# Values of six more blocks' late rows in the opening, and first-MLP products of two token groups in the slots that this frees

## The chip, the cores and the metric

The kernel runs on one core of one Trainium2 chip. A core has a matrix engine (PE), a vector engine (DVE), a scalar engine (ACT), a general engine (POOL), a sync engine that issues most transfers (SP), and 16 DMA engines. The metric is the device time of one execution in microseconds (us); three runs of the kernel before gave 797.42, 798.40 and 799.69 us, median 798.4.

## The reference

A recurrent attention layer over segments, then an MLP, on 2048 tokens of width 512 in bf16:

```python
h  = x  + A(_layernorm(x))      # A: 64 segments of 32 tokens, 32 heads of 128, 8 memory tokens
h2 = h  + B(_layernorm(h))      # B: layernorm, w1 (512x1792), gelu, w2 (1792x512)
# A, for segment s:
hcat = concat([mem, xs])        # 8 + 32 rows
q, k, v = hcat@Wq, hcat@Wk, hcat@Wv        # each 512 -> 32*128
p = softmax(mask(q k^T * 128**-0.5))       # memory columns always seen, the rest causal
o = (p v) @ Wo                              # 4096 -> 512
mem = o[:, :8]; out rows = o[:, 8:]
```

Segment s+1 needs `mem` of segment s, so the 64 segments form a chain. What does not depend on `mem` can be computed at any time before its use.

## The kernel before

All work is recorded as operations with estimated durations; a list scheduler in the program then sets the order on each engine, and semaphores follow from it. The order on PE is written by hand: per segment a table `ORDERS` of parts (Q, K, V passes, scores SC, values times weights PV, output projection WO, scores for the token rows SA), with one filler part `F`. `START` is the hand-written order for segment 0, the opening, in which the four weights (4 MB each) arrive from DRAM in the order WV, WK, WQ, WO.

Of each segment's 32 rows the first 24 sit beside the 8 memory rows in the tile `hT`. The last 8 rows ("late rows") of four segments together form a block's 32 late rows; they do not depend on memory. A block is four segments (16 blocks, `bk = s // 4`, `sg = s % 4`). The late rows' keys, queries and values are made by passes of their own: a pass multiplies 32 rows by 2048 weight columns in 16 matmuls, so values of one block are two passes. The opening makes them for blocks 0 and 1. For the later blocks `part_F2`, the filler of each segment, makes those of block `bk + 2`: keys in `sg` 0, queries in 1, values in 2; `sg` 3 holds the output projection of the late rows (`wo_B`). Values leave PSUM to `VSB`, go to the DRAM tensor `v_last` (`v_B_spread`) and return to `VBD` in another layout (`v_B_gather`).

In blocks 14 and 15 no late rows are left, so the six free fillers hold the start of the MLP: `w1_pair(p, banks)` makes two 128-wide column groups (`fc`) of the first MLP product for the first 512 tokens (token group k=0). There are 14 column groups, seven pairs; pairs 0 to 5 are in these slots, pair 6 comes after the last segment. Their w1 columns are loaded early (`w1_early`, by the table `EARLY`), the products stay in SBUF where tiles are free (`gT0_home`), and `gelu` runs on them in place once the last softmax is done.

After the segments the MLP runs over token groups k = 0 to 3 of 512 tokens: `p2_w1` (128-wide column group, four matmuls of 512 columns) with gelu on ACT, and `p2_w2` (four matmuls per column group). The tiles of WK, WQ and WV are then reused for w1, w2, gelu results, layernormed rows. `p2_load` reads the rows h of a group from DRAM, `p2_norm` and `p2_T` normalize and transpose them (DMA transposes), `p2_res` adds the bias on POOL, `nat(bk)` brings a block's attention output into rows. POOL folds the two halves of `wo_B` (`fold`). All these transfers stand in one in-order queue, SP's.

The program also spaces transfers around PE's instruction fetches and pads PE's instruction stream (`windows`, `pads`); both are computed anew for every version.

## Time and profile before

| what | value |
|---|---|
| median of three runs | 798.4 us (797.42 to 799.69) |
| the profiled execution, device time | 797.54 us |
| its span, first to last instruction | 795.8 us |
| mean granted PE clock | 0.993 |
| PE busy | 765.4 us, 96% of the span |
| DVE, ACT, POOL busy | 585.3, 530.0, 308.1 us |
| moved by DMA | 48.02 MB |

The span falls into three stretches: the opening to 51.7 us (weights arrive, segment 0), the segments 1 to 63 to about 696 us, and the MLP. A number after L is a line of the kernel before; `high` and `quad` are the two halves of PSUM. In the rows of PE, `128*32` is the stationary operand and the number behind `x` counts matmuls; four matmuls with 32 stationary columns each run side by side. Idle time of PE is what can be won without taking work away from it; the profile names for each such wait what ended it.

### The profile page before, as it was taken

The numbers are of one execution on the slowest core, as the hardware profiler recorded it, in microseconds if no ns is written. First come the engines' busy times: TensorE is split into PE (matmuls) and PEld (weight loads), VectorE is DVE, ScalarE is ACT, GpSimd is POOL, SyncE is SP. The second block draws the span as 40 slices with busy tenths as digits, with TensorE's granted clock in tenths as the row PEclk, the third lists the DMA queues.
The fourth block names the chain that finished last, engine by engine and source line by source line (L and its number), as shares of the span: only waits on it lengthen the run. The fifth ranks groups of instructions, "written<-read, shape, count | busy, mean of one in ns | idle before, by whom it ended". The sixth has DMA issues, their size and how long they took to land.

```text
span 795.8 us, 45330 instructions
## 1 busy us (share of the span) xinstructions
PE 765.4 (96%) x19686; PEld 424.7 (53%) x20409; DVE 585.3 (74%) x1862; ACT 530.0 (67%) x1380; POOL 308.1 (39%) x831
## 2 busy tenths in 40 slices
PE   3789999999999999999999999999999999989998
PEld 1345555565665555555555555565655566544443
DVE  4258788888888888888888888888888787834111
ACT  2447777777777777677777777777677677743432
POOL 3013223434343444444444444444452434335600
PEclk9989999999999999999999999999999999999999
DMA  9951000010102010201010101010103211274300
GB/s 338 395 182 24 17 14 26 18 44 11 44 10 57 4 47 14 45 17 38 23 38 23 38 25 36 25 38 23 37 21 80 56 31 44 80 211 106 80 26 27
DMA packets 65056, 48.02 MB, mean 60 GB/s; under 512 B 28500, under 2 KB 61276, under 8 KB 64860
## 3 DMA queue, kind: packets, MB, share of 16 engines
q1 hardware_dynamic: 64528, 44.85, 19.6%
q8 instruction: 158, 2.59, 1.4%
q10 hardware_dynamic: 332, 0.27, 0.2%
q14 instruction: 38, 0.31, 0.1%
HBM read 31.08 MB, written 8.13 MB: 49 GB/s over the span
## 4 chain that ended last, share of the span: by engine, by line
PE 90%; SPq 5%; DMA 2%; DVE 1%; issue 1%; ACT 0%; DVEq 0%
PE high L957 33%; PE high L700 17%; PE quad L1287 15%; PE quad L1677 6%; PE high L1670 5%; PE high L1326 3%; SPq L860 2%; SPq L878 2%; PE quad L1140 2%; PE quad L1197 2%; PE quad L1247 2%; PE quad L1171 1%; PE high L1171 1%; PE high L1487 1%; DMA WO<-in_A_Wo_dram 1%; DMA WQ<-h_mid 1%
## 5 line engine op out<-in xcount | busy, mean ns | idle before, releaser
L957 PE MATMUL high<-WQ,hT 128*32 128x512 bf16 x1796 | 157.5, 383 | 1.6 <-DVE hT L1293 1.0
L700 PE MATMUL high<-WK,hT 128*32 128x512 bf16 x1260 | 126.4, 379 | 0.1
L1220 POOL TENSOR_TENSOR PA<-SA,rsa 128x256 bf16<-128x256 f32 x64 | 39.6, 619 | 219.9 <-DVE rsa L1212 152.6
L1287 PE MATMUL quad<-WO,OT 128*32 128x256 bf16 x4032 | 122.1, 273 | 0.0
L957 PE MATMUL high<-WV,hT 128*32 128x512 bf16 x1528 | 115.9, 380 | 0.0
L976 ACT ACTIVATE kq<-high 128x512 bf16<-128x512 f32 x160 | 94.1, 597 | 22.6 <-PE high L957 19.0
L975 ACT CAST kq<-high 128x512 bf16<-128x512 f32 x161 | 93.7, 582 | 21.5 <-PE high L957 19.8
L1287 PEld LDWEIGHTS quad<-WO,OT 128*32 128x32 bf16 x4032 | 102.3, 97 | 5.0 <-issue 0.2
L1228 POOL COPY BD<-PTA 32x128 f32<-32x128 f32 x256 | 78.3, 306 | 16.3 <-DVE PTA L1224 0.6
L957 PEld LDWEIGHTS high<-WQ,hT 128*32 128x32 bf16 x1796 | 52.0, 95 | 54.8 <-issue 22.9
L998 DVE STREAM_TRANSPOSE KALL<-kq 128x256 f32<-128x256 f32 x160 | 69.3, 433 | 9.7 <-ACT kq L975 7.0
L975 ACT CAST VS<-high 128x512 bf16<-128x512 f32 x126 | 73.1, 580 | 0.1
L955 PEld LDWEIGHTS <-hT 128*32 128x32 bf16 x3248 | 53.1, 97 | 35.1 <-DVE hT L1293 7.0
L1673 ACT ACTIVATE WQ<-high,b1t 128x512 bf16<-128x512 f32 x42 | 28.9, 687 | 54.6 <-PE high L1670 54.6
L975 ACT CAST OT<-quad 128x384 bf16<-128x384 f32 (+1 forms) x126 | 47.3, 375 | 26.3 <-PE quad L1175 25.2
L1299 DVE STREAM_TRANSPOSE TT<-quad 128x256 f32<-128x256 f32 x63 | 28.3, 450 | 42.0 <-PE quad L1287 41.5
L1034 ACT COPY KALL<-KALL 128x128 f32<-128x128 f32 x63 | 18.8, 298 | 58.9 <-PE quad L1197 58.7
L1339 POOL TENSOR_TENSOR opT<-TTB,TTS 32x64 bf16<-32x64 f32 x128 | 40.3, 315 | 40.6 <-DVE opT L1293 22.8
L998 DVE STREAM_TRANSPOSE QT<-kq 128x256 f32<-128x256 f32 x128 | 54.5, 426 | 2.0 <-ACT kq L976 1.8
L957 PE MATMUL high<-WK,hT 128*32 128x512 bf16 x788 | 55.1, 379 | 0.0
L1140 PEld LDWEIGHTS quad<-KALL,ZC 128*32 128x32 bf16 x1984 | 31.2, 96 | 41.3 <-POOL BD L1228 17.4
L700 PE MATMUL high<-WV,hT 128*32 128x512 bf16 x520 | 53.1, 379 | 0.0
(188 smaller groups left out, 1612.3 us busy)
## 6 DMA issues: line engine op xcount, KB each, us to landing
WV<-in_A_Wv_dram SPq DMA_DIRECT2D x4, 1024.0 KB, 10.1
WK<-in_A_Wk_dram SPq DMA_DIRECT2D x4, 1024.0 KB, 18.3
WQ<-in_A_Wq_dram SPq DMA_DIRECT2D x4, 1024.0 KB, 17.6
WO<-in_A_Wo_dram SPq DMA_DIRECT2D x16, 256.0 KB, 7.9
v_last<-VSB SPq DMA_DIRECT2D x60, 64.0 KB, 2.3
VBD<-v_last SPq DMA_DIRECT2D x60, 64.0 KB, 2.0
h_mid<-xr SPq DMA_DIRECT2D x16, 128.0 KB, 2.0
WQ<-h_mid SPq DMA_DIRECT2D x4, 512.0 KB, 5.7
```

What stands on the lines that cost most here:

```text
L700: return e.add_instruction(mybir.InstMatmult(name="I-%d" % (4000000 + _kept[0]), engine=mybir.EngineType.PE, start_tensor_calc=start, stop ...
L955: e.ldweights(l, tile_position=(0, 32 * j))
L957: ins = e.matmul(o, l, m, start=(k == 0), stop=(k == DC - 1), tile_position=(0, 32 * j), skip_group_check=True)
L975: return {"act": (lambda e: e.copy(out, src), t_act(n, ps_)), "dve": (lambda e: e.tensor_copy(out, src), 0.155 + 1.0e-3 * n * fast)}
L976: return {"act": (lambda e: e.mul(out, src, scale_), t_act(n, ps_)), "dve": (lambda e: e.tensor_scalar(out, src, scale_, None, ALU.mult), ...
L998: S.op("dve", lambda e: e.transpose(out, src), reads=[("kq", i)], writes=[key], dur=t_dve(256) + 0.02)
L1140: ins = e.matmul(o[32 * j:32 * j + 32, :], zc_window(h), rhs, start=False, stop=(i == 3), tile_position=(0, 32 * j), skip_group_check=True)
L1228: S.narrow(S.op("pool", lambda e, j=j, rows=rows: e.tensor_copy(words(BD[rows, par, :, j, :, :]), words(PTA[rows, 0:4])), reads=["PTA"], w ...
L1287: ins = e.matmul(ps[bank][32 * j:32 * j + 32, 0:256], lhs(slot(h)), wo_cols(h, b), start=(k == 0), stop=(k == 15), tile_position=(0, 32 * ...
L1339: return e.tensor_tensor(o[32 * q:32 * q + 32, c:c + 2], x, y, ALU.add)
L1670: ins = e.matmul(ps[bank][:, 0:SBT], W1[:, cc, fc * P:(fc + 1) * P], hnT_of(k)[:, cc, :], start=(cc == 0), stop=(cc == DC - 1))
L1677: S.op("pe", lambda e: e.matmul(quad[:, t, c0:c0 + w], gT_of(k, fc)[:, t * P:(t + 1) * P], W2[:, fc, c0:c0 + w], start=(fc == (0 if k else ...
```

## The change

The values of blocks 2 to 7 are made in the opening as well (12 more passes, all from WV), and `part_F2` then makes those of block `bk + 8`. The value slots of blocks 8 to 13 become free: with the six of blocks 14 and 15 there are twelve slots. They take all seven pairs of token group 0 and five pairs (10 of 14 column groups) of token group 1. The products no longer stay in SBUF: each pair is copied to `kq[4:6]`, stored to a DRAM tensor `g_pre` (256 KB) and loaded back after the last segment. Before the values of blocks 2 to 6 can go to DRAM they wait in tiles that are free early (`stages`); the transfers follow in segments 2 to 6.

The late rows of four blocks are now loaded together as one tile (`load_xl`, `ln_late`, tiles `hL`), the ring `hT` holds 3 blocks and not 4, `xr` 5 and not 6, `VS` 2 segments and not 3, `BD` and `BDL` one and not two. `ln1` runs two blocks ahead and not three. The normalized rows of group 0 get a tile of their own, `hn0`, filled around segments 24 to 32; those of group 1 are made around segments 53 to 56.

After the segments, group 0 has only its second product, and group 1 four column groups of the first (10 to 13) and its second product; groups 2 and 3 are as before.

```diff
+VL = 8
+SLOTS = tuple(s for s in range(4, 64) if s % 4 < 3 and s // 4 + (VL if s % 4 == 2 else 2) >= 16)
+NP1 = len(SLOTS) - 7
+EARLY = {2: (("vs", 4, 0.1),), 3: (("vs", 2, 0.1),), 4: (("vs", 3, 0.1),), 5: (("vs", 5, 0.1), ("xl", 3, 0.5)), 6: (("vs", 6, 0.1),),
...
-        RBLK = 4
+        RBLK = 3
...
-        XR = 6
+        XR = 5
...
-        VS = sb("VS", [P, 3, 2, 512])
+        VS = sb("VS", [P, 2, 2, 512])
...
-        BD = sb("BD", [P, 2, 4, 4, SEG, 2])
-        BDL = sb("BDL", [P, 2, 2, 8, 8])
+        BD = sb("BD", [P, 4, 4, SEG, 2])
+        BDL = sb("BDL", [P, 2, 8, 8])
...
         load_x(0, first)
+        load_xl(0, first)
...
-        load_x(1, first)
+        load_xl(1, first)
         load_w(WV, wv_d, "WV")
         load_w(WK, wk_d, "WK")
-        load_x(2, load)
         load_w(WQ, wq_d, "WQ")
...
-        load_x(3, load)
...
+        stages = {1: (halves(opT[:].rearrange("p a c t -> p (a c t)")), [("opA", p_, k) for p_ in range(2) for k in range(4)] + [("opB", p_) for p_ in range(2)]),
+                  2: (halves(xr[:, 3:5, :].rearrange("p a d -> p (a d)")), [("xr", 3), ("xr", 4)]),
+                  3: (halves(TTB[:].rearrange("p c q t -> p (c q t)").bitcast(BF16)), ["TTB"]),
+                  4: (halves(OTB[:, 1].rearrange("p h t -> p (h t)")), [("OTB", 1, sg) for sg in range(4)]),
+                  5: (halves(h0[:, 0:1024]), [("hn0", "a")]),
+                  6: (halves(h0[:, 1024:2048]), [("hn0", "b")])}
...
             def part_F2():
                 banks = BANK["F0"], BANK["F1"]
-                to = bk + AHEAD - 1
                 what = (1, 2, 0)[sg - 1] if bk == 0 else sg
+                to = bk + (VL if what == 2 else AHEAD - 1)
...
-                    w1_pair(3 * (to - NTB) + what, banks)
+                    w1_pair(SLOTS.index(s), banks)
...
-            g, gkeys = gT0_home[p]
-            for n in range(2):
-                S.either(copy2(g[:, n, :], ps[banks[n]][:, 0:SBT], SBT), reads=[("ps", banks[n])], writes=[("W1o", n), ("gT0", 2 * p + n)] + gkeys)
+            o = kq[:, 4:6].rearrange("p i a e b -> p i (a e b)")
+            for a in range(2):
+                S.either(copy2(o[:, a, :], ps[banks[a]][:, 0:SBT], SBT), reads=[("ps", banks[a])], writes=[("W1o", a), ("kq", 4 + a)])
+            S.dma(lambda e: e.dma_start(gd[k, p], o.rearrange("p a n -> p (a n)")), 256, reads=[("kq", 4), ("kq", 5)], writes=[("gd", k, p)])
...
+        for p in range(NP):
+            gT_load(0, p)
+            f = slice(2 * p, 2 * p + 2)
+            S.dma(lambda e, f=f: e.dma_start(W2[:, f], w2_d[:, f]), 256, writes=[("W2", p)], after=used["WK"])
+        p2_load(0)
...
+        for p in range(NP1):
+            gT_load(1, p)
+        w1_load(1)
+        p2_load(1)
+        w1_load(0)
...
-        w1_pair(NP - 1, early)
-        for fc in range(FC):
-            gelu(fc)
+        for fc in range(FC):
+            gelu(0, fc)
         wo(NS, later, mem=False)
-        rest = {0: lambda: nat(NTB - 2), 1: lambda: (pv_a(NS - 1), pv_a_ev(NS - 1)), 3: lambda: (wo_B(NTB - 1, later), fold(14)), 5: lambda: (wo(NS + 1, 7, mem=False), nat(NTB - 1))}
+        rest = {0: lambda: nat(NTB - 2), 1: lambda: (pv_a(NS - 1), pv_a_ev(NS - 1)), 4: lambda: (wo_B(NTB - 1, later), fold(14)), 6: lambda: (wo(NS + 1, 7, mem=False), nat(NTB - 1))}
...
+        for fc in range(2 * NP1):
+            gelu(1, fc)
+        p2_norm(2)
+        p2_T(2)
...
+        for fc in range(2 * NP1, FC):
+            p2_w1(1, fc)
+        for fc in range(FC - lag):
+            p2_w2(1, fc)
+        finish(1)
+        for k in (2, 3):
```

The order of instructions at three places, before and after. PE in the opening, before (`XX` holds the late rows; L957 is a pass of 16 matmuls per half, L905 a transpose, L1076 the turn of block 0's values, L1140 scores):

```order
L957 MATMUL high<-WV,XX 32x512 x32
L957 MATMUL high<-WK,XX 32x512 x32
L957 MATMUL high<-WK,hT 32x512 x32
L957 MATMUL high<-WK,XX 32x512 x32
L957 MATMUL high<-WQ,XX 32x512 x16
L905 MATMUL quad<-ident,XX 128x128 x4
L957 MATMUL high<-WQ,hT 32x512 x16
L957 MATMUL high<-WQ,XX 32x512 x16
L957 MATMUL high<-WQ,hT 32x512 x16
L1140 MATMUL high<-KALL,ZC 32x64 x32
```

and after, from the turn of block 0's values on (L979 is the pass, L913 the transpose; `XX` holds the late rows of blocks 0 to 3, `hL` those of blocks 4 to 7):

```order
L1116 MATMUL quad<-VSB,OTB 128x256 x16
L979 MATMUL quad<-WV,XX 32x512 x32
L979 MATMUL high<-WK,XX 32x512 x16
L979 MATMUL high<-WK,hT 32x512 x16
L979 MATMUL high<-WK,XX 32x512 x16
L913 MATMUL quad<-ident,XX 128x128 x4
L979 MATMUL quad<-WV,hL 32x512 x32
L979 MATMUL high<-WK,XX 32x512 x16
L979 MATMUL high<-WK,hT 32x512 x16
L979 MATMUL high<-WK,XX 32x512 x16
L979 MATMUL quad<-WV,hL 32x512 x48
L979 MATMUL high<-WQ,hT 32x512 x16
```

Value passes now stand between the passes that need the weights which arrive later. PE at the end of the segments, before (L1326 is `wo_B`, L1487 `w1_pair`, L1287 WO, L1677 the second MLP product, L1247 and L1253 the last values times weights):

```order
L1287 MATMUL quad<-WO,OT 32x256 x64
L1326 MATMUL high<-WO,OTB 32x512 x16
L1487 MATMUL high<-XX,hT 32x512 x16
L1487 MATMUL high<-XX,xr 32x512 x16
L1287 MATMUL high<-WO,OT 32x256 x64
L1677 MATMUL quad<-WK,xr 128x512 x4
L1247 MATMUL high<-BD,VS 128x2x32 x16
L1253 MATMUL high<-BDL,VBD 128x8x8 x4
L1677 MATMUL quad<-WK,xr 128x512 x4
L1677 MATMUL quad<-WK,VSB 128x512 x4
L1326 MATMUL high<-WO,OTB 32x512 x32
```

and after (L1366 is `wo_B`, L1327 WO, L1735 the second product, L1287 and L1293 the last values times weights, L1728 the first product):

```order
L1327 MATMUL quad<-WO,OT 32x256 x64
L1366 MATMUL high<-WO,OTB 32x512 x16
L1327 MATMUL high<-WO,OT 32x256 x64
L1735 MATMUL quad<-WK,WQ 128x512 x4
L1287 MATMUL high<-BD,VS 128x2x32 x16
L1293 MATMUL high<-BDL,VBD 128x8x8 x4
L1735 MATMUL quad<-WK,WQ 128x512 x12
L1366 MATMUL high<-WO,OTB 32x512 x32
L1735 MATMUL quad<-WK,WQ 128x512 x8
L1327 MATMUL high<-WO,OT 32x256 x64
L1735 MATMUL quad<-WK,WQ 128x512 x32
L1728 MATMUL high<-XX,WK 128x512 x16
```

Pair 6 is gone from between `wo_B` and WO, the next `wo_B` has one column group of the second product more ahead of it, and only 16 matmuls of the first product follow for group 1. SP's queue at the same place, before (L1688 loads w2, L1693 w1, L1421 rows of h, L1438 transposes rows, L1357 is `nat`):

```order
L1695 DMA WQ<-in_B_b_dram 128x512
L1688 DMA WK<-in_B_w_dram 128x2x512 x5
L1421 DMA WQ<-h_mid 128x2048
L1688 DMA WK<-in_B_w_dram 128x2x512 x2
L1693 DMA WK<-in_B_w_dram 128x896
L1438 DMA_TRANSPOSE WQ<-WV 128x4x128 x4
L1693 DMA WK<-in_B_w_dram 128x896 x3
```

and after (L1522 loads the stored products, L1765 w2, L1745 w1, L1458 rows of h, L1397 is `nat`):

```order
L1522 DMA WQ<-g_pre 128x1024 x6
L1765 DMA WK<-in_B_w_dram 128x2x512 x5
L1522 DMA WQ<-g_pre 128x1024
L1765 DMA WK<-in_B_w_dram 128x2x512 x2
L1745 DMA WK<-in_B_w_dram 128x896 x4
L1458 DMA WQ<-h_mid 128x2048
L1767 DMA WQ<-in_B_b_dram 128x512
L1522 DMA KALL<-g_pre 128x1024 x4
L1397 DMA_TRANSPOSE oN<-opT 128x4x128
L1522 DMA KALL<-g_pre 128x1024
L1745 DMA WK<-in_B_w_dram 128x896 x3
L1458 DMA WQ<-h_mid 128x2048
```

Six loads of 256 KB now stand ahead of the first load of w2, and the rest of group 1's products, half of w1 and the rows of groups 1 and 2 stand behind `nat` of block 14.

More of the change, by code (lines that the diff above doesn't have):

```diff
@@ new lines, in build_kernel, with w1_home, w1_early @@
+        homes = [(VSB[:].rearrange("p i r e -> p (i r e)"), [("VSB", 0), ("VSB", 1)]),
+                 (QTB[:, 13 % AHEAD].rearrange("p h t b -> p (h t b)"), [("QTB", 13 % AHEAD, r) for r in range(2)])]
+        def w1_home(n):
+            late = sum(s >= NS - 7 for s in SLOTS[:n + 1])
+            v, keys = homes[late % 2]
+            return v.rearrange("p (c f) -> p c f", c=DC), keys
+        def w1_early(n, after):
+            v, keys = w1_home(n)
+            p = n % NP
+            for c in range(DC):
+                S.dma(lambda e, c=c: e.dma_start(v[:, c, :], w1_d[:, c, 2 * p * P:(2 * p + 2) * P]), 64, writes=[("W1p", n, c)], after=after + S.users(keys))
@@ new lines, in gT_key, with gT_load, gelu @@
+        def gT_key(k, fc):
+            return ("gT1" if k == 1 else "gT", fc)
+        def gT_load(k, p):
+            o = gT[:, 2 * p:2 * p + 2, :] if k == 0 else KG[:, 2 * p:2 * p + 2, :]
+            S.dma(lambda e: e.dma_start(o.rearrange("p a n -> p (a n)"), gd[k, p]), 256, reads=[("gd", k, p)], writes=[gT_key(k, 2 * p + n) for n in range(2)], after=used["KG"] if k else used["WQ"])
+        def gelu(k, fc):
+            g, key = gT_of(k, fc), gT_key(k, fc)
+            start = k == 0 and fc == 0
+            S.op("act", lambda e: e.activation(g, g, ACTF.Gelu_apprx_tanh, bias=b1t[:, fc:fc + 1], scale=1.0), reads=[key, "b1t"], writes=[key],
+                 dur=0.65 + 1.1 * start, after=[S.last_writer["SA"], S.last_writer[("EC", 1)]] + ([] if start else [S.last_writer[("gT", 0)]]))
@@ L1559, in tail @@
                 if folds:
-                    fold(n, behind + [S.last_writer[("BD", s % 2, j)] for j in range(4 * (s == NS - 1))])
-                if turned and s % 4 == 3:
+                    fold(n, behind + [S.last_writer[("BD", j)] for j in range(4 * (s == NS - 1))])
+                if turned and (s % 4 == 3 or s == NS - 10):
                     for f in turned:
@@ L1646, in build_kernel @@
                 tail(0)
-                chain += spread["out", 1] + spread["in", 1]
+                load_xl(2, load)
+                load_x(1, load)
+                chain += spread["out", 1] + spread["in", 1] + spread["out", VL - 1]
                 for a_, b_ in zip(chain, chain[1:]):
@@ L1663, in build_kernel @@
             used[key] += S.users([(key, r, c_) for r in range(2) for c_ in range(DC)])
+        used["KG"] = S.users([("KA", p_, r) for p_ in range(2) for r in range(2)] + [("KB", p_, r) for p_ in range(AHEAD) for r in range(2)] + [("KL", p_) for p_ in range(2)])
+        used["QG"] = S.users([("QTB", p_, r) for p_ in range(AHEAD) for r in range(2)])
         def p2_w1(k, fc):
@@ L1727, in build_kernel @@
                 for c in range(parts):
-                    for fc in (range(FC - lag, FC) if k else ORDER0[FC - lag:]):
+                    for fc in range(FC - lag, FC):
                         p2_w2t(k, fc, t, c * w, w)
                     cols = slice(c * w, c * w + w)
-                    S.op("dve", lambda e, t=t, bf=bf, cols=cols: e.tensor_tensor(ob[:, bf, t, cols], quad[:, t, cols], hb[:, bf, t, cols], ALU.add),
-                         reads=[("ps", t), ("hb", bf, t)], writes=[("ob", bf, t, c)], after=used["WV"], dur=t_dve(w))
@@ new lines, in build_kernel @@
+        wo(NS, later, mem=False)
+        rest = {0: lambda: nat(NTB - 2), 1: lambda: (pv_a(NS - 1), pv_a_ev(NS - 1)), 4: lambda: (wo_B(NTB - 1, later), fold(14)), 6: lambda: (wo(NS + 1, 7, mem=False), nat(NTB - 1))}
+        p2_res(0)
+        p2_load(2)
+        for fc in range(FC - lag):
+            rest.get(fc, lambda: None)()
+            p2_w2(0, fc)
+        finish(0)
+        for fc in range(2 * NP1):
+            gelu(1, fc)
+        p2_norm(2)
+        p2_T(2)
+        p2_res(1)
+        p2_load(3)
@@ L1734, in build_kernel @@
+        for fc in range(2 * NP1, FC):
+            p2_w1(1, fc)
+        for fc in range(FC - lag):
+            p2_w2(1, fc)
+        finish(1)
+        for k in (2, 3):
+            for fc in range(FC):
+                p2_w1(k, fc)
+                if fc >= lag:
+                    p2_w2(k, fc - lag)
+                if fc == 8:
+                    p2_res(k)
+                if fc == 8 and k == 2:
+                    p2_norm(3)
+                    p2_T(3)
+            finish(k)
         S.op("sp", lambda e: e.nop(), reads=[("out", tb, c) for tb in range(NTB) for c in range(1 + (tb == NTB - 1))])
```

272 lines of the change are left out of this document (129 added, 143 removed), and 7 rows, old and new, of tables (EARLY, START).

## The prediction

> **What bounds the kernel now.** I read the page's busy times and slices first, then what PE waited for in each of the three stretches, then the chain of work that ended last in the opening.
>
> ```profile
> span 795.8 us, 45330 instructions
> PE 765.4 (96%) x19686; PEld 424.7 (53%) x20409; DVE 585.3 (74%) x1862; ACT 530.0 (67%) x1380; POOL 308.1 (39%) x831
> PE   3789999999999999999999999999999999989998
> PEclk9989999999999999999999999999999999999999
> GB/s 338 395 182 24 17 14 26 18 44 11 44 10 57 4 47 14 45 17 38 23 38 23 38 25 36 25 38 23 37 21 80 56 31 44 80 211 106 80 26 27
> ```
>
> PE is the bound from the fourth slice on: only the first three slices, in which 338 and 395 GB/s of weights come in, leave it idle, and one near the end. A matmul that leaves the later slices is worth its full time; one put into the first slices may be free. The waits, by stretch (0 to 52, 52 to 690 and 690 to 796 us, in this order):
>
> ```profile
> PE high L957 <- DMA WQ<-in_A_Wq_dram: 3.5, 3, 2.0
> PE high L957 <- DMA WK<-in_A_Wk_dram: 1.5, 1, 1.5
> ...
> PE high L1487 <- DMA VSB<-in_B_w_dram: 1.7, 1, 1.7
> PE quad L1197 <- issue: 1.4, 6, 0.3
> ...
> PE high L1287 <- issue: 0.8, 1, 0.8
> PE high L1326 <- DVE OTB L975: 0.7, 1, 0.7
> ```
>
> In 638 us of segments PE waits a few us, and 1.7 of them once, for the w1 columns of the first pair. In the opening it is the reverse, and there the chain shows what ends it:
>
> ```profile
> 40.20 8.04 DMA WO<-in_A_Wo_dram
> ...
> 50.41 0.36 PE high L1287 x8
> ...
> 51.72 0.39 PE high L957
> ```
>
> Up to 48.2 us the chain is WO arriving; segment 1 begins at 51.72. PE work added before that point moves the end only if PE is then later than WO.
>
> **The change, part by part.** *What leaves the MLP.* PE from the last segment on:
>
> ```profile
> 696.87 1.04 PE L1487 MATMUL high<-XX,hT 128*32 128x512 bf16 x16
> 697.74 1.04 PE L1487 MATMUL high<-XX,xr 128*32 128x512 bf16 x16
> 698.60 0.71 PE L1287 MATMUL high<-WO,OT 128*32 128x256 bf16 x17
> ...
> 709.46 1.93 PE L1287 MATMUL high<-WO,OT 128*32 128x256 bf16 x64
> ...
> 719.11 4.66 PE L1670 MATMUL high<-WQ,WK 128*128 128x512 bf16 x19
> 723.60 1.03 PE L1677 MATMUL quad<-WK,WQ 128*128 128x512 bf16 x4
> ...
> 725.33 1.03 PE L1677 MATMUL quad<-WK,WQ 128*128 128x512 bf16 x4
> ```
>
> From 723.60 to 725.33 PE does one column group of the second product and one of the first, so a group is 0.865 us. Ten groups of token group 1 leave: 8.65 us. Pair 6 leaves the place between 696.87 and 698.60: 1.73 us. Both lie on the path. In the freed slots a pair replaces the two value passes of a block, which take as long:
>
> ```profile
> 21.55 1.91 PE L957 MATMUL high<-WV,XX 128*32 128x512 bf16 x32
> 23.28 1.47 PE L957 MATMUL high<-WK,XX 128*32 128x512 bf16 x24
> ```
>
> 21.55 to 23.28 is 1.73 us for a block's values. So the segments keep their length, and the added work of six blocks is 6 x 1.73 = 10.4 us, all in the opening.
>
> *What the opening has room for.* By stretches (PE busy is the second time, the granted clock the third number from the end):
>
> ```profile
> 17.00:27.00 10.00, 7.58 (x120) 3.77 (x104) 2.23 (x4) 3.98 (x9) 0.00 (x0) 1.00 1.03 408
> 27.00:37.00 10.00, 6.49 (x114) 2.44 (x105) 4.05 (x11) 5.30 (x12) 0.79 (x2) 1.00 1.03 398
> 37.10:47.30 10.20, 8.33 (x176) 4.40 (x170) 4.82 (x16) 4.78 (x14) 0.00 (x0) 0.51 1.10 348
> ...
> L975 ACT CAST VS<-high 128x512 bf16<-128x512 f32 x126 | 73.1, 580 | 0.1
> ```
>
> Idle are 2.4 + 3.5 + 1.9 = 7.8 us. In the third stretch the clock is at half, so its 8.3 busy us are some 4.2 us of work: 4.1 us more room if the clock stays up. That is 11.9 us for 10.4, and the new value passes need WV alone, which is there first, while the waits above were for WK and WQ. Their evacuations go to ACT, 12 x 0.58 = 7.0 us (last row), and ACT is busy only 3.98 and 5.30 of 10 us there. What stays tight is the chain of segment 0 behind the last Q pass. WO itself comes a little sooner: one x load of 128 KB fewer is ahead of it in the queue, at 348 GB/s 0.4 us. I take -0.4; the bounds are -1.0 (the rest of the idle before 50.41 gone too) and +3.5 (below).
>
> The clock is the doubtful part. It fell at 37.1 us, after ten us in which PE was 65% busy and the longest listed wait for WQ was 2.0 us, so partial idleness was enough. The Trainium skill ("TensorE: Matmul & The Clock Gate", Part 1: The HAM clock gate) says that half rate comes back after at least one idle window of about 3.4 us; the trace does not agree, with its 2.0 us. By that rule the fuller opening could not lose its clock, and the sum would stand without the first rival. From the rows alone: the ten us before would now be filled with value passes, so the fall is unlikely, but the chain of segment 0 keeps its short waits.
>
> *The one wait in the segments.* The first pair stood in segment 56 and its columns went to VSB, which held block 15's values from segment 54 on, so the load came late. Now the values of block 15 are made in segment 30, the first pair comes in 34 and its load by `EARLY` from 31 on; the later ones are loaded about three segments ahead in blocks 9 to 13 and at least one in 14 and 15. I take the whole 1.7 us off (bounds 0 and 1.7).
>
> *The hand-over to the MLP.* Without pair 6 the steps follow sooner on each other, so I ask what each then waits for:
>
> ```profile
> 698.07 1.33 POOL L1228 COPY BD<-PTA 32x128 f32<-32x128 f32 x4
> 696.53 1.48 ACT L1476 ACTIVATE xr<-xr,b1t 128x512 bf16<-128x512 bf16 x2
> 690.26 0.33 SPq L1695 DMA_DIRECT2D WQ<-in_B_b_dram  x1
> ...
> 692.00:694.00 2.00, 2.00 (x74) 1.05 (x68) 0.89 (x2) 1.36 (x3) 0.86 (x3) 1.00 0.78 214
> 694.00:696.00 2.00, 2.00 (x84) 1.92 (x82) 1.83 (x6) 1.62 (x3) 0.00 (x0) 1.00 0.97 322
> 696.00:698.00 2.00, 2.00 (x48) 1.02 (x43) 1.86 (x5) 1.96 (x4) 1.01 (x2) 1.00 1.06 321
> ...
> DMA to landing us min/median/max: 3.3/4.8/7.3
> ```
>
> PE would start WO at 696.87 and end it by 698.8 (1.93 us at most, row 709.46), do the first group until 699.6 and then the last values times weights, whose operand BD is complete at 699.4: no wait. The next `wo_B` has four groups of the second product ahead of it and not three, 0.86 us more, so the 0.7 us wait for OTB goes. Transfers into WQ's place could start at 690.3 (third row). Six product loads (1.57 MB) now stand ahead of w2; at 321 GB/s, moving from about 692, the first w2 piece (1.84 MB in all) is there at 697.7, and up to 1 us later as landings go (last row, the w2 loads). It is needed at 698.8: I take a 0.5 us wait, bounds 0 and 2 us (at the 214 GB/s of the start all along: 700.6). Later pieces come every 0.8 us and are used every 1.73 us. The gelus began at 696.5; their first products then lie there, loaded since 690.3. The 0.8 us of "issue" I leave as it is. Together -0.2 us.
>
> *Group 2's rows.* Group 0's second product would end at 719.1 - 1.7 - 0.2 = 717.2, and group 1 takes (4 + 14) x 0.865 = 15.6 us, before 24.2 (28 groups). So group 2 starts at 732.8. Ahead of it stand in SP's queue `nat` of block 14, which waits for POOL's fold, and `p2_res` on POOL, which frees the tile for the rows:
>
> ```profile
> 707.64 1.48 POOL L1339 TENSOR_TENSOR opT<-TTB,TTS 32x64 bf16<-32x64 f32 x4
> ...
> L1433 POOL TENSOR_TENSOR WV<-WQ x16: 1143/1151/1336, 716.4 to 750.3; 128x512 f32<-128x512 bf16 x16
> ...
> DMA to landing us min/median/max: 3.8/5.7/6.9
> ...
> 700.54 1.46 DVE L1427 TENSOR_SCALAR WV<-WQ,agg,rst 128x512 bf16<-128x512 bf16 x4 [2.42 <-DMA WQ<-h_mid]
> 726.04 5.13 SPq L1438 DMA_TRANSPOSE WQ<-WV x4
> ```
>
> Block 14's fold ended at 709.1; I put it at 710. Four adds of 1.15 end at 714.6, the rows (third row, their landing) are there at 718.4 to 721.5, normalized at 719.9 to 723.0, and the four transposes issued by 725.0 to 728.1, with up to 3 us to land. The cover is 1.7 us in the worst of these and 5 in the best, so I cost it at nothing; rows later than that would stall PE directly.
>
> *The smaller buffers and extra transfers in the segments.* BD once instead of twice: it is written at 698.07, last read at
>
> ```profile
> 693.85 0.41 PE L1247 MATMUL quad<-BD,VS 64*128 64x64 bf16 x16
> ```
>
> so four us apart; VS in two copies is read by the following segment only, before its own successor is written. Neither has to wait. What I cannot see is how the new spacing of transfers meets PE's instruction fetches: the issue waits of 1.4 us may vanish or double and more. I take +0.6, near the small end, since pairs stand in the slots of blocks 14 and 15 already and the slices there show PE at 9 too; bounds -1.4 and +2.
>
> The sum: -8.65 - 1.73 (MLP) - 0.4 (opening) - 1.7 (VSB) - 0.2 (hand-over) + 0.6 (segments) = -12.1 us. The profiled execution took 797.54 us (span 795.8), 0.9 below the median of the runs and inside them. 797.5 - 12.1 = 785.4; against the median it would be 786.3. I forecast 785.5.
>
> **The rivals.** *The opening overruns.* If a half-clock stretch of 10 us stays, the segment-0 chain behind the fuller passes ends later: the 4.1 us of room are missing, 7.8 remain for 10.4 us of work, so 2.6 us, and about 1 more since the chain of segment 0 is itself at half clock: +3.5 to +4, 789.5. For it: the clock fell without a long wait. Against it: the waits before 37 us, which made it fall, are where the value passes go.
>
> *The MLP waits for SP's queue.* w2 behind the products, or group 2's rows behind `nat` and `p2_res`: 2 us either way, 787.5. For it: 3.1 MB more go through one in-order queue in that stretch. Against: the covers worked out above.
>
> *The segments get longer (slower than before).* A single BD, two VS or a block less of lead put a wait into every segment, or a 256 KB store into a fetch. The gain of 12.1 us is lost at 12.1 / 63 = 0.19 us per segment; at 0.3 us the time is 804. For it: PE has no slack in the segments, its slices show 9 throughout. Against: BD and VS are 4 us apart and more, and the transfers per block stay alike (256 KB of w1 in and 256 KB of products out, 256 KB of values less).
>
> *The values in the opening are not hidden at all.* Then +10.4 on the sum: 795.8, within 0.3% of the profiled execution. Only if PE were already the limit there, which the chain denies.
>
> **How the numbers follow.** Forecast 0.63; opening overruns 0.18; MLP waits 0.10; segments longer 0.05; nothing hidden 0.04. The range: at the low end every stall of the hand-over gone and the opening 1 us shorter, 782.5; at the high end the overrun with the 2 us of the second rival and some of the fetch waits, 792.5. It leaves out the last two and the corners of the others, under 2 in 10. A change under 0.3% (2.4 us) could not be told from none. Faster: 0.91 (the first three); the same: 0.04; slower: 0.05.
>
> **What would show it.** Right: segment 1 starting at 51 to 52 us with PE 9 in the second slice and no half clock before 47; segments of the same length, no wait for w1 columns; the stretch from block 14's `wo_B` to group 1's first product about 2 us shorter; group 1 taking 15.6 us. Wrong: a start of segment 1 after 53; issue or BD waits repeated in each segment; PE waiting for w2 or for group 2's transposes.

## The result, and the profile after

The changed kernel takes 786.87 us (median of four runs, 785.56 to 787.22), the kernel before 798.07 us beside it (four runs, 797.42 to 799.69): a ratio of 0.9854, 95% interval 0.9835 to 0.9873, so 11.2 us or 1.5% faster. One run of the kernel before, among the eleven beside the last four versions below, took 1279.24 us at a granted clock of 0.56 and is left out of the ratios. The profiled execution took 786.69 us against 797.54, 10.85 us less. The page of the changed kernel:

```profile
span 784.9 us, 45522 instructions
PE 763.3 (97%) x19817; PEld 426.4 (54%) x20393; DVE 591.6 (75%) x1873; ACT 533.8 (68%) x1387; POOL 309.9 (39%) x829
PE   4989999999999999999999999999999999999998
PEclk9999999999999999999999999999999999999999
GB/s 327 398 220 71 60 23 34 11 43 12 47 15 38 24 45 37 44 38 58 30 52 24 51 24 44 31 44 30 32 43 52 87 63 37 51 270 255 87 35 27
```

PE is busy 2.1 us less than before, in a span 10.9 us shorter. The second and third slices went from 7 and 8 to 9 and 8, and the clock has no 8 left. The same three stretches of the opening as in the prediction, and what PE waited for in it (0 to 52 us), with the first data still on its way left out:

```profile
17.00:27.00 10.00, 10.00 (x172) 5.22 (x168) 0.52 (x2) 6.44 (x11) 0.00 (x0) 1.00 1.03 410
27.00:37.00 10.00, 9.32 (x176) 4.48 (x170) 3.42 (x8) 5.91 (x11) 0.34 (x1) 1.00 1.03 401
37.10:47.30 10.20, 9.04 (x251) 5.05 (x241) 6.99 (x20) 6.89 (x20) 0.00 (x0) 1.00 1.10 349
...
PE high L979 <- DVE hT L1333: 1.0, 1, 1.0
PE high L1327 <- DMA WO<-in_A_Wo_dram: 0.9, 2, 0.5
PE quad L979 <- ACT hL L997: 0.7, 1, 0.7
PE quad L1211 <- DVE PTC L1197: 0.7, 1, 0.7
```

Of the 7.8 us of idle time 1.8 are left, and the clock is 1.00 throughout (0.51 before in the third stretch). The waits for WK and WQ are gone; two short ones for WO are there. The chain of waits ends the opening as before, on the same transfer:

```profile
41.29 7.65 DMA WO<-in_A_Wo_dram
...
50.45 0.36 PE high L1327 x8
...
51.76 0.40 PE high L979 x4
```

Segment 1 begins at 51.76 us, and it began at 51.72. Waits in the segments (52 to 690 us), and after them (690 to 786):

```profile
PE quad L1327 <- issue: 1.2, 1, 1.2
PE quad L1237 <- issue: 1.1, 4, 0.3
...
PE high L1327 <- DVE TTB L1370: 1.2, 1, 1.2
```

The 1.7 us for the first pair's w1 columns are gone, and so are the 0.7 for OTB after the segments. New are 1.2 of "issue" in one segment and 1.2 at the hand-over, for VectorE's read of PSUM. The timeline of PE there (start, duration, operation):

```profile
696.44 1.04 PE L1366 MATMUL high<-WO,OTB 128*32 128x512 bf16 x16
698.70 1.93 PE L1327 MATMUL high<-WO,OT 128*32 128x256 bf16 x64 [1.22 <-DVE TTB L1370]
700.56 1.04 PE L1735 MATMUL quad<-WK,WQ 128*128 128x512 bf16 x4
...
717.08 3.71 PE L1728 MATMUL high<-XX,WK 128*128 128x512 bf16 x16
...
732.71 2.63 PE L1728 MATMUL high<-WQ,WK 128*128 128x512 bf16 x11
```

So token group 1 goes from 717.08 to 732.71. From the two timelines, in us, after minus before (a stretch ends where the next begins):

| stretch | before | after | difference | predicted |
|---|---|---|---|---|
| to segment 1's first product | 51.72 | 51.76 | +0.04 | -0.4 |
| segment 1 to segment 63, first products | 635.72 | 636.12 | +0.40 | -1.1 |
| segment 63 to the last `wo_B` | 8.57 | 8.56 | -0.01 | 0 |
| last `wo_B` to group 1 (hand-over) | 23.10 | 20.64 | -2.46 | -1.93 |
| token group 1 | 24.35 | 15.63 | -8.72 | -8.65 |
| groups 2, 3 and the end | 52.33 | 52.19 | -0.14 | 0 |
| sum | | | -10.89 | -12.1 |

Where the segments are compared below, their time runs from segment 1's to segment 63's scores for the token rows (L1237 after): 631.93 us before, 632.32 after. It is the same stretch, 3.8 us shorter at its ends.

### The profile page after: what moved, and what is told of

Read it like the earlier page. It is cut to its first block, busy times and chain, and to the rows that moved or that the text cites. A ratio compares the mean times of both kernels' runs of the same rounds, so it can differ in the third digit from the quotient of the medians.

```text
span 784.9 us, 45522 instructions
## 1 busy us (share of the span) xinstructions
PE 763.3 (97%) x19817; PEld 426.4 (54%) x20393; DVE 591.6 (75%) x1873; ACT 533.8 (68%) x1387; POOL 309.9 (39%) x829
## 4 chain that ended last, share of the span: by engine, by line
PE 92%; SPq 5%; DMA 1%; issue 1%; DVE 0%; ACT 0%; DVEq 0%
PE high L979 33%; PE high L705 17%; PE quad L1327 15%; PE quad L1735 6%; PE high L1728 4%; PE high L1366 3%; PE high L1537 3%; SPq L891 3%; SPq L867 2%; PE quad L1180 2%; PE quad L1237 2%; PE quad L1287 2%; PE quad L1211 2%; PE high L1211 1%; DMA WO<-in_A_Wo_dram 1%
## 5 line engine op out<-in xcount | busy, mean ns | idle before, releaser
L979 PE MATMUL high<-WQ,hT 128*32 128x512 bf16 x1796 | 158.5, 380 | 1.5 <-DVE hT L1333 1.0
L705 PE MATMUL high<-WK,hT 128*32 128x512 bf16 x1260 | 128.8, 379 | 0.2 <-issue 0.2
L1327 PE MATMUL quad<-WO,OT 128*32 128x256 bf16 x4032 | 122.0, 273 | 1.2 <-issue 1.2
L997 ACT CAST kq<-high 128x512 bf16<-128x512 f32 x182 | 104.9, 583 | 24.0 <-PE high L979 18.6
L979 PE MATMUL high<-WV,hT 128*32 128x512 bf16 x1544 | 117.9, 381 | 0.0
L1327 PEld LDWEIGHTS quad<-WO,OT 128*32 128x32 bf16 x4032 | 102.2, 97 | 6.3 <-issue 1.5
L979 PEld LDWEIGHTS high<-WQ,hT 128*32 128x32 bf16 x1796 | 53.5, 95 | 55.5 <-issue 23.0
L977 PEld LDWEIGHTS <-hT 128*32 128x32 bf16 x3056 | 50.6, 96 | 34.5 <-DVE hT L1333 7.2
L997 ACT CAST OT<-quad 128x128 bf16<-128x128 f32 (+1 forms) x127 | 47.5, 374 | 24.9 <-PE quad L1215 23.9
L979 PE MATMUL high<-WK,hT 128*32 128x512 bf16 x788 | 56.2, 379 | 0.0
L705 PE MATMUL high<-WV,hT 128*32 128x512 bf16 x504 | 52.9, 379 | 0.0
L979 PEld LDWEIGHTS high<-WV,hT 128*32 128x32 bf16 x1544 | 36.8, 96 | 26.5 <-issue 20.0
## 6 DMA issues: line engine op xcount, KB each, us to landing
WV<-in_A_Wv_dram SPq DMA_DIRECT2D x4, 1024.0 KB, 10.9
```

Source lines behind the costliest of these rows:

```text
L705: return e.add_instruction(mybir.InstMatmult(name="I-%d" % (4000000 + _kept[0]), engine=mybir.EngineType.PE, start_tensor_calc=start, stop ...
L977: e.ldweights(l, tile_position=(0, 32 * j))
L979: ins = e.matmul(o, l, m, start=(k == 0), stop=(k == DC - 1), tile_position=(0, 32 * j), skip_group_check=True)
L997: return {"act": (lambda e: e.copy(out, src), t_act(n, ps_)), "dve": (lambda e: e.tensor_copy(out, src), 0.155 + 1.0e-3 * n * fast)}
L1327: ins = e.matmul(ps[bank][32 * j:32 * j + 32, 0:256], lhs(slot(h)), wo_cols(h, b), start=(k == 0), stop=(k == 15), tile_position=(0, 32 * ...
```

## The experiments

**The opening with less work, and with more.** The first edit lets the added value passes run one contraction step of four, the second adds idle matmuls:

```diff
-            one_pass(*pack_b(bk), WV, "WV", r, bank, cols_v, back)
+            passes(*pack_b(bk)[:2], [(WV, "WV", r, bank, cols_v)], back, pack_b(bk)[2], 1 if bk > 1 else 4)
```

> The opening's value passes for the late rows of blocks 2 to 7 run one of their four contraction steps, so about 10.4 x 3/4 = 7.8 us of TensorE work is left out and those values are wrong by the missing steps. If the added passes fill time in which TensorE waited anyway, the first segment starts where it does in the changed kernel (51.76 us, within 1 us), and the granted clock falls below 1.00 somewhere before 47 us, as in the kernel before. If they take TensorE's time, the first segment starts up to 7.8 us sooner, at about 44 us, and the run takes about 779 us; half of each would be 783.

```diff
...
-("B", "V", 6, (0, 0)), "Q0",
+("B", "V", 6, (0, 0)), ("W", 2, 16), "Q0",
...
```

> 16 matmuls of 128x512 whose result nobody reads (3.45 us of TensorE) are added in the opening, ahead of the first query projection; nothing is left out. If the opening of the changed kernel still has room (0.9 us of waits for the output weights, 0.7 and 0.7 for evictions), the first segment starts about 1.7 us later, at 53.5 us, and the run takes 788.6 us. If TensorE's work alone sets the opening's end, it starts 3.45 us later, at 55.2 us, and the run takes 790.3. If the added passes were all free because another chain sets the end, it stays within 0.5 us of 51.8.

With thinner passes segment 1 began at 51.92 us, 0.16 later than in the changed kernel, though 7.8 us of work were gone. The waits (0 to 52 us) and four stretches say where they went:

```profile
PE high L979 <- DMA WQ<-in_A_Wq_dram: 3.4, 2, 1.7
PE high L1327 <- DMA WO<-in_A_Wo_dram: 3.0, 3, 1.1
...
17.00:27.00 10.00, 9.31 (x148) 4.59 (x132) 4.47 (x8) 6.32 (x11) 0.00 (x0) 1.00 1.02 408
27.00:37.00 10.00, 6.81 (x132) 2.92 (x128) 5.20 (x14) 5.89 (x13) 0.34 (x1) 1.00 1.03 401
37.00:46.00 9.00, 5.23 (x152) 2.63 (x152) 5.18 (x14) 3.95 (x12) 0.00 (x0) 1.00 1.10 350
46.00:50.00 4.00, 3.36 (x22) 0.96 (x23) 0.00 (x0) 0.00 (x0) 0.00 (x0) 0.57 1.05 308
```

The wait for WQ is back, that for WO is three times as long, and after 9 us in which PE was 58% busy the clock falls, to 0.57 in the mean of the next four. The added passes were free: they fill idle time behind transfers that run at 350 to 410 GB/s either way. The run took 790.84 us in spite of that; its segments took 635.69 us, 3.4 more than the changed kernel's with the same work in them (see the repeat below).

With 16 idle matmuls segment 1 began at 55.16 us, 3.40 later:

```profile
53.78 0.40 PE L1327 MATMUL high<-WO,OT 128*32 128x256 bf16 x8
55.16 0.40 PE L979 MATMUL high<-WQ,hT 128*32 128x512 bf16 x4 [0.98 <-DVE hT L1333]
```

No wait for WO is left, and PE is now what ends the opening. The 3.40 us are nearly the full 3.45 and not the 1.7 of the theory with slack, but in part by chance: 0.92 of them stand ahead of the added work, since the first pass with `hL` began at 29.86 us, and at 28.94 in the changed kernel's profile. Behind it the way to segment 1 became 2.47 us longer, so about 1 us of the added work took the place of the 0.9 us for WO. The other waits of that opening, 0.7 us for `hL` and 0.7 for the probabilities (`PTC`), are there again (0.7 and 0.6): the first stands ahead of the added work, the second moved with its chain. So the change filled the opening up to the wait for WO: less work wins nothing, more work costs its time beyond that wait. (791.95 us in one run.)

In all ten profiles with the same value passes and no work added (the changed kernel's own, its repeat and eight of the edits, one of them without the last idle matmuls), segment 1 began 1.51 to 1.52 us after the last piece of WO had landed (at 49.58 to 50.25 us, by its issue and its time to landing). In the two of the kernel before it was 2.14 and 1.97 us, and with thinner passes 2.27, behind the half clock.

**The pairs thinner, and thicker.** The pairs of the six freed slots run one contraction step of four, or their first column group twice:

```diff
-            for cc in range(DC):
+            steps = 1 if n < 6 else DC
+            for cc in range(steps):
```

> The pairs of the six slots of blocks 8 to 13 run one of their four contraction steps, so 6 x 1.3 = 7.8 us of TensorE work is left out of the segments and those first-MLP products are wrong by the missing steps. If TensorE's work sets the segments' length, seven to eight us are gained: from segment 1's start to segment 63's 636.1 becomes about 628.3 and the run takes 779. If the pairs stand where TensorE would wait for the chain through softmax anyway, the segments stay at 635 to 636 and the run at 786.

```diff
-                    for a in range(2):
+                    for a in (0, 0, 1) if n < 6 else (0, 1):
```

> The pairs of the six slots of blocks 8 to 13 run a half more matmuls (the first column group twice, so its products are wrong): 6 x 4 x 8 matmuls, 5.2 us of TensorE work more. With thinner pairs the segments had not become shorter (632.8 against 632.3 us), so without them TensorE waits for the normalised rows; if the pairs of the changed kernel fill that wait exactly, each matmul more costs its full time and the segments take 637.5 us. If the wait is longer than the pairs, the segments stay within 1 us of 632.3, and a pair of six steps would have been free.

7.8 us less work changed nothing: the segments took 632.83 us (632.32), the run 788.20. PE's waits in the segments:

```profile
PE high L979 <- DVE hT L1333: 4.6, 6, 0.8
PE high L1211 <- DVE PTC L1197: 1.6, 6, 0.3
```

Six waits each, one for each thin pair, 6.2 us in all: for the memory rows of the next segment (`hT`), which come out of the chain through softmax and output projection, and for `PTC` before that. The changed kernel has neither in its segments. With half a pair more, 5.2 us of work, the segments took 633.85 us, 1.53 more. By place: the six stretches that hold a pair and the six after them take 123.82 us thin, 123.87 as changed (124.20 in the repeat below) and 126.16 thick. In the other profiles with the pairs as they are it is 122.8 to 125.0 us, so the thick pairs stand out and the thin ones do not. So the chain of a segment and PE's work with a pair are nearly equal in length; the pairs are free since they stand where PE would otherwise wait, and above them each matmul begins to cost, not all of it here.

**The bank at the hand-over.** `wo` of the last segment and `wo_B` of block 14 both used PSUM bank `later`, 4. Pair 6 stood between them.

```diff
-        wo(NS, later, mem=False)
+        wo(NS, 6, mem=False)
```

> The output projection of the last segment writes PSUM bank 6 in place of bank 4, which the projection of block 14 used just before; nothing is left out. If the new wait of 1.22 us at 698.7 us (TensorE for VectorE's read of bank 4) is the bank's, it is gone and from block 14's projection to token group 1's first product the time falls from 20.64 to 19.4 us; the run takes 785.5. If something else ends up late there (the normalised output of the last segment, the eviction that follows), the wait moves and the 20.64 stays within 0.4 us.

The wait for TTB is gone, but the hand-over became longer, 23.53 us (20.64), and the run 789.77:

```profile
PE quad L1735 <- DMA WK<-in_B_w_dram: 2.6, 1, 2.6
...
699.40:702.00 2.60, 0.01 (x3) 0.00 (x0) 0.45 (x1) 2.60 (x5) 2.19 (x6) 1.00 1.05 345
702.00:703.00 1.00, 0.96 (x5) 0.33 (x6) 0.00 (x0) 1.00 (x3) 0.82 (x3) 1.00 1.09 379
703.00:706.50 3.50, 3.50 (x28) 1.58 (x28) 1.45 (x3) 3.02 (x5) 2.93 (x8) 0.51 1.07 385
706.50:708.00 1.50, 1.50 (x14) 0.58 (x16) 0.00 (x0) 0.00 (x0) 0.14 (x1) 1.00 0.99 223
```

PE now arrives 1.2 us sooner at group 0's second product, and the first w2 piece is not there until 702.04: 2.63 us of idle time, and then some 3.4 us at half clock (the third number from the end). In SP's queue the w2 pieces stood behind seven loads of 256 KB from `g_pre`:

```profile
690.88 4.10 SPq L1522 DMA_DIRECT2D WQ<-g_pre  x7
695.03 4.32 SPq L1765 DMA_DIRECT2D WK<-in_B_w_dram  x7
```

The edit had moved this too: in the changed kernel six loads stood ahead of the first w2 piece, which was issued at 693.98 us and landed 6.2 us later, at 700.2; here it was issued at 695.03 and landed 6.9 us later. So not all of the 2.63 us would have stood behind the bank's wait in the changed kernel. The next run issues the first w2 piece behind the first of the loads:

```diff
-        def gT_load(k, p):
+        def gT_load(k, p, behind=None):
...
-            gT_load(0, p)
+            gT_load(0, p, S.last_writer.get(("W2", 0)) if p else None)
```

> The projection of the last segment writes bank 6 as in the run before, and the first piece of the second MLP weights goes ahead of the stored first-MLP products on SP's queue, from the second of these on; nothing is left out. In the run with bank 6 alone TensorE waited 2.63 us for that piece and its clock was then halved for 3.5 us. If the issue behind seven loads is why it was late, both are gone, and from block 14's projection to token group 1's first product it takes 19.4 us (20.64 in the changed kernel, 23.5 with bank 6 alone); the run takes about 785.5. If the transfers themselves are the limit, the wait moves to the next pieces and the stretch stays at 20.6 or more.

Both waits are gone:

```profile
696.32 1.04 PE L1366 MATMUL high<-WO,OTB 128*32 128x512 bf16 x16
...
699.03 1.04 PE L1735 MATMUL quad<-WK,WQ 128*128 128x512 bf16 x4
...
700.87 0.31 PE L1287 MATMUL high<-BD,VS 64*128 64x64 bf16 x9 [0.57 <-issue]
...
716.31 3.71 PE L1728 MATMUL high<-XX,WK 128*128 128x512 bf16 x16
```

The hand-over took 19.99 us, of which 0.57 are an "issue" wait; without it 19.42, as expected. The run took 785.90.

**Where the 1.7 us of the first pair's wait went.** The kernel before, with the load at the start of segment 56:

```diff
...
-56: (("hn", 2, 0.1), ("hn", 3, 0.3), ("w1", 0, 0.5)),
+56: (("hn", 2, 0.1), ("hn", 3, 0.3), ("w1", 0, 0.02)),
...
```

> The kernel before, with the load of its first pair's weights issued at the start of segment 56 and not in its middle; nothing is left out. If the 1.66 us wait at 621.9 us is the late issue of that load on SP's queue, segment 55's 12.06 us fall to about 10.3 and the time from segment 1's start to segment 63's from 631.9 to 630.2 us. If the wait was worth nothing because the next one takes its place, segments 56 and 57 grow by as much and the sum stays within 0.5 us of 631.9.

The wait is gone and its stretch falls from 12.06 to 10.66 us, but the segments together took 632.30 us against 631.93. No wait of its kind took its place; instead the waits that the profile calls issue came differently in the whole program (the two largest of PE's waits in the segments):

```profile
PE quad L1197 <- issue: 2.0, 6, 0.4
PE high L1326 <- issue: 0.6, 1, 0.6
```

So neither theory holds: the neighbours did not grow, the gain was lost in stretches far away (segments 14 and 18, for example, 0.80 and 0.47 us longer). The issue waits rose from 2.2 to 2.9 us in sum; that is less than half of the 1.8 us lost (the 1.4 won there and 0.4 more), and what makes the rest no view shows. The run took 797.99 us.

**Are the long stretches due to the stores?**

```diff
-            S.dma(lambda e: e.dma_start(o.rearrange("p a n -> p (a n)"), gd[k, p]), 256, reads=[("gd", k, p)], writes=[gT_key(k, 2 * p + n) for n in range(2)], after=used["KG"] if k else used["WQ"])
+            S.dma(lambda e: e.dma_start(o, w2_d[:, 2 * p:2 * p + 2]), 256, writes=[gT_key(k, 2 * p + n) for n in range(2)], after=used["KG"] if k else used["WQ"])
...
-            S.dma(lambda e: e.dma_start(gd[k, p], o.rearrange("p a n -> p (a n)")), 256, reads=[("kq", 4), ("kq", 5)], writes=[("gd", k, p)])
```

> The changed kernel without the twelve stores of first-MLP products to DRAM; the loads that fetched them read as many bytes of the second MLP weights, so the MLP of token groups 0 and 1 computes with wrong values. If the segments' stretches over 10.4 us (the profile of the changed kernel has nine, mostly in the segment after a pair) come from the stores' traffic, which delays TensorE's instruction fetch, the time from segment 1's start to segment 63's falls from 632.3 to about 629 us, since the nine lie 4.7 us above the floor of 10.09 in sum. If they come from something else (the fetch meets other loads, or the vector chain is late there), it stays at 632 to 633.

No: 633.07 us without a store, with other stretches long (12, 28, 34, 43), and a run of 786.83 us.

**The pairs of group 1 not used, the changed kernel again, and two versions timed.**

```diff
-        for p in range(NP1):
-            gT_load(1, p)
...
-        for fc in range(2 * NP1):
-            gelu(1, fc)
...
-        for fc in range(2 * NP1, FC):
+        for fc in range(FC):
             p2_w1(1, fc)
```

> The changed kernel, but token group 1 computes all of its first MLP itself, as 16 column groups of 0.866 us: the five pairs made for it in the segments are stored and not used, their five loads are left out. Opening, segments and hand-over keep their instructions. If the gain lies in group 1's shorter list alone, group 1 takes 24.3 us again (15.63 in the changed kernel) and the run 795.5, near the kernel before. If a part of the gain is in the opening or in the segments, the run stays 2 us or more under the kernel before on this chip.

> The changed kernel once more, nothing edited. If TensorE's short fetch stalls belong to the program's layout, the long segments are the same ones as in its first profile (6, 35, 38, 42, 46, 51, 60, 61, to 0.1 us each) and segment 1 to segment 63 takes 632.3 us. If they come by chance of timing, they fall into other segments, and the sum moves by up to a microsecond.

> The version with bank 6 and the first piece of the second MLP weights sooner, unchanged, now timed. Its one profile ended at 785.9 us, its hand-over 0.65 us shorter than the changed kernel's. If that holds, it is 0.5 to 0.9 us faster than the changed kernel run beside it; if the stalls elsewhere take it back, the two agree within 0.3 us.

```diff
...
-("T", "WO", 6, 7), ("W", 7, 4), ("T", "WO", 7, 8))
+("T", "WO", 6, 7), ("T", "WO", 7, 8))
```

> The same version without the last four idle matmuls of the opening (0.86 us, ahead of the last piece of the first output projection); nothing is left out of the result. If the output weights' last piece has landed by then, segment 1 starts up to 0.86 us sooner. If the transfer sets the opening's end, TensorE waits for it in place of them, segment 1 starts within 0.2 us of where it did (60.5 us on the same scale as 61.2 for the changed kernel), and the clock is what to watch.

These four ran on one chip. With the pairs unused the run took 793.65 us, 6.7 over the changed kernel's median there (786.95) and 2.8 under the kernel before (796.48). Group 1:

```profile
714.87 12.87 PE L1728 MATMUL high<-XX,WK 128*128 128x512 bf16 x56
...
739.66 2.63 PE L1728 MATMUL high<-WQ,WK 128*128 128x512 bf16 x11
```

714.87 to 739.66 is 24.79 us, 9.2 more than with the pairs and 0.4 more than before (x56 is 14 column groups of four matmuls; the 16 of the expectation are a slip). The rest of what it keeps against the kernel before is its hand-over (21.19 us against 23.10) and segments that came out short in this one program, 630.15 us. So group 1's shorter list is most of the gain, and the opening gives nothing by itself.

The changed kernel's repeat took 786.95 us (six runs, 784.38 to 788.48; ratio 0.9876, 0.9855 to 0.9898). Its hand-over had the same 1.2 us wait for TTB and took 20.65 us; the segments took 631.79 us, 0.53 less than in the first profile. Of the eight long stretches named, that of 38 came again to 0.1 us (10.73) and that of 61 with 0.3 us more (11.64); 35 and 51 were shorter than they had been (10.61 and 10.35), 6, 42, 46 and 60 were at 10.1 to 10.2, and others were longer (34: 10.99). The long one is at the same instruction of segment 61 in both; here is the repeat's, which answers to the 1.2 us above:

```profile
684.26 1.82 PE L1327 MATMUL quad<-WO,OT 128*32 128x256 bf16 x60 [1.43 <-issue]
```

So part of these waits is the program's layout, part chance. That they are waits for instructions is only argued: the profile names nothing that ends them. Nor do they make up the differences between runs: PE's listed waits in the segments come to 3.1 us in the changed kernel and to 3.3 with the thin values, whose segments took 3.4 us more. With the pairs thin, thick, unstored or unused, the other edits and the repeat, the segments took 630.15 to 635.69 us, and no run explains that spread by work.

The version with bank 6 and the sooner w2 piece took 786.91 us (five runs, 784.90 to 787.47; ratio 0.9869, 0.9847 to 0.9891), the same as the changed kernel within what can be told. Its hand-over was 19.24 us in this profile, but in segment 60 PE waited once for ScalarE and then ran at half clock (the wait, the 3.4 us in which it lies and the 3.4 after them):

```profile
PE quad L1327 <- ACT quad L1157: 1.7, 1, 1.7
...
672.37:675.79 3.42, 1.76 (x68) 1.17 (x60) 1.86 (x7) 2.44 (x9) 1.55 (x5) 1.00 0.08 26
675.79:679.20 3.41, 3.41 (x68) 2.58 (x61) 0.37 (x1) 0.00 (x0) 0.28 (x1) 0.50 0.02 5
```

The stretch of segment 60 took 13.62 us, and the segments 635.20 (632.86 in this version's first profile). Why ScalarE's mask copy came late there stays open.

Without the last four idle matmuls of the opening PE waited 1.2 us for WO in their place,

```profile
49.87 0.40 PE L1327 MATMUL high<-WO,OT 128*32 128x256 bf16 x8 [1.21 <-DMA WO<-in_A_Wo_dram]
51.24 0.40 PE L979 MATMUL high<-WQ,hT 128*32 128x512 bf16 x4 [0.98 <-DVE hT L1333]
```

and segment 1 began at 51.24 us, 0.14 later than with them (51.10): the transfer sets that end. The clock stayed at 1.00 there. Its six runs spread from 784.38 to 790.55 us (median 788.33, ratio 0.9889, 0.9860 to 0.9918); the profile is of a run of 785.0. The three slower ones, 789.76 to 790.55, are those with a mean granted clock of 0.998, the other three have 1.0. One fall of 3.4 us to half clock would make that difference (an estimate: half of 3.4 in 787 us is 0.002), so each of them probably had one; where, and what else made them slower, was not seen. No version was measurably faster than the changed kernel.

## Why the prediction was right, and which terms were mis-sized

**The MLP's shorter list, -8.65.** Right in mechanism and size: -8.72, and without the pairs' use group 1 takes 24.79 us again. The 1.73 us of pair 6 is not measured alone; it is in the hand-over below.

**The opening hides 10.4 us, and begins segment 1 0.4 us sooner.** The first half is right, and the two edits show it from both sides: 7.8 us less moved the start by +0.16, 3.45 more by +3.40. My room of 11.9 us against 10.4 left 1.5, and 1.8 us of idle time are in fact left. But at most the 0.9 us for WO of it took the second edit's work: I counted every idle time as room, and the waits for `hL` and `PTC` stay. The small gain did not come in the profile above (+0.04): the WO transfer in the chain landed at 48.94 us, and at 48.24 before, so the x load fewer ahead of it did not bring it sooner. Over the ten profiles with this opening the start lay between 51.09 and 51.76, in the mean at 51.38, against 51.72 and 51.58 in the two of the kernel before. So about 0.3 us may have come, not from an earlier WO but since PE no longer was late behind it; the spread is as large.

**The clock stays up.** Right, and the thinner passes show that it was the passes that kept it up. Here the row and the Trainium skill ("TensorE: Matmul & The Clock Gate", Part 1: The HAM clock gate) still differ. Its rule, half rate after at least one idle window of about 3.4 us, would not have let the clock fall after the idle times of 2.63 us and of 1.7 us, and it fell after both. It stayed at half for 3.41 us each time, which does agree with a window of 3.4 us.

The traces show what decides. Within a profile the changes of the clock lie whole multiples of 3.41 us apart: in the kernel before it fell at 37.20 us and rose at 47.44, three times 3.41 later. Cut at that spacing, these are the 3.41 us ahead of that fall, and, with the thinner passes, a stretch that no fall followed and the one ahead of the fall at 46.22 us (PE busy is the second time):

```profile
33.79:37.20 3.41, 1.05 (x16) 0.35 (x20) 0.45 (x1) 0.94 (x3) 0.00 (x0) 1.00 1.05 375
35.98:39.39 3.41, 1.69 (x28) 0.66 (x28) 1.89 (x6) 1.53 (x4) 0.00 (x0) 1.00 1.10 352
42.81:46.22 3.41, 0.81 (x16) 0.30 (x16) 1.44 (x4) 0.47 (x1) 0.00 (x0) 1.00 1.10 349
```

In all the profiles together the clock fell six times before the end of the program, and in the 3.41 us ahead of each PE was busy for 0.81 to 1.76 us; the 1.76 are in the row with the wait for ScalarE above. No fall followed a stretch with 1.81 us or more, nor three with 1.69 to 1.74. So by these rows it is the busy share in a fixed stretch of 3.41 us that decides, not the length of one wait, and the border is near a half. The TTB wait of 1.22 us lay in a stretch with 2.19 us busy. At half clock it took more to come back: behind 2.16 and 2.80 us busy (the kernel before, from 37.20 and 40.62 us) the clock stayed at half, behind 2.94 and more it rose. Where the steps lie differs from run to run: the clock first rose at 16.45 us in the changed kernel's profile and at 18.28 with the thin pairs, and the pass that ran meanwhile, 32 matmuls from 16.1 us on, took 2.09 us in the one and 2.98 in the other. How much of the opening before ran at half clock was thus partly chance: with the sooner w1 load, which leaves the work of the opening as it was, it was 6.8 us and not 10.2, and segment 1 began 0.14 us sooner (51.58).

**The VSB wait, -1.7, and the segments' fetches, +0.6.** The step that failed. The wait did go, but the segments became 0.4 us longer and not 1.1 shorter. The same wait taken out of the kernel before also left the segments at +0.4 (632.30 against 631.93). What I costed as a gain on a path is worth nothing that this measurement can tell, because the segments move by -2 to +3 us from one version to the next. That this comes from how every edit lays PE's instruction stream and its transfers out anew is argued, not shown. The bounds that I gave for that unknown, -1.4 and +2, were too narrow: seen were -2.2 and +3.4 against the changed kernel's first profile.

**The same length of the segments with a pair in a freed slot.** Right, but the reason was incomplete. I argued that PE is the limit there and a pair takes as long as the two value passes. PE had no slack only since the slot was full: with three quarters of the pairs' work gone the time stayed, and PE waited 6.2 us for the chain instead.

**The hand-over, -0.2 besides pair 6.** Near in sum (-1.93 predicted with pair 6, -2.46 measured), wrong in its parts, so that the sum came near is in part luck. The OTB wait of 0.7 went as said. The 0.8 us of "issue" that I left in went as well, with some smaller ones. The 0.5 us wait for the first w2 piece did not come, since a wait for a PSUM bank, 1.22 us, came before it: I looked for operands that would be late and not for the bank that the two projections share, which pair 6 had given time to be read. The piece itself landed at 700.2 us in this profile, where I had put it at 697.7 from bytes and bandwidth, and up to 1 us later; in the repeat it landed 5.2 us after its issue at 692.62, at 697.8. Without the bank's wait PE would have come to it 1.22 us sooner than 700.56, at 699.3, and waited 0.8 us (an estimate from these rows), and in the repeat not at all. So my 0.5 us, with bounds of 0 and 2, was not far off. The 2.63 us of the run with bank 6 lie above them, but there the piece was issued a microsecond later, behind one load more.

**Group 2's rows.** Right: forecast 732.8 us for their first use, measured 732.71 without a wait. Their transposes:

```profile
720.28 5.13 SPq L1475 DMA_TRANSPOSE WQ<-WV  x4
```

The last was issued by 725.4 (725.0 to 728.1 forecast), and they landed at most 3.3 us after their issue, so at least 4 us of the cover were left.

**The rivals.** The overrun of the opening and longer segments did not happen; the second edit shows how near the first was, since 3.5 us more work there would have made it so. The rival of SP's queue came near as well: the first w2 piece landed 0.4 us before PE used it.

## What to carry to other kernels

A slot in which an engine would wait is worth as much work as the wait is long. Move work into time that transfers already set, give the freed slot something that another stage is bound by, and the gain is read in that last stage alone: here 8.7 us from 10.4 moved, with nothing to be seen where it was moved. When an instruction is taken from between two others, ask not only which operands the second needs but which buffer both write. And before fixing one wait, look at what stands right behind it: here the fix of 1.2 us alone cost 2.9, part of it since it changed the queue's order too; with the next transfer moved as well the hand-over was 0.7 and 1.4 us shorter in two profiles, and the whole run no faster that could be told.

## What the hardware did that was not expected

In these profiles the granted clock changed only at fixed steps of 3.41 us, and fell to half for one step or more when PE had been busy for about half of the step before or less (0.81 to 1.76 us of 3.41 in the six falls). So a single idle time of 1.7 us was enough where it lay whole within one step; 1.2 us were not. A fall for one step costs 1.7 us of work (an estimate: half of 3.41), so a wait of 1.7 us costs up to twice its length. And the same program took 632.3 and 631.8 us for the same segments, another version 632.9 and 635.2, with ScalarE's late copy in the second: differences of a microsecond or two in a stretch of 630 say nothing of an edit unless the rows show the wait itself.
